# A down product with 20 products over four token tiles, three feature groups and two column halves, in a fused state-space and feed-forward kernel on one core

## The chip, the core and the metric

The kernel runs on one core of a Trainium2 chip. A core has five engines that each work through a list of instructions in order: TensorE (PE, matrix products; its weight loads are a row of their own, PEld), VectorE (DVE), ScalarE (ACT, functions from a table that has to be loaded), GpSimd (POOL) and SyncE (SP, which here only issues transfers). They wait for each other by semaphores. The metric is the device time of one execution in microseconds (us), less is better.

## What is computed

A chunked state-space recurrence (4 batches, 8 heads, 768 positions, head dimension 32, state 16) gives 3072 tokens of 256 values. These go through a feed-forward layer with 1536 hidden features, all in fp32:

```python
rms = np.sqrt(np.mean(x * x, axis=-1, keepdims=True) + 1e-06)
xn = x / rms * rms_g
g = xn @ w_gate                          # 256 x 1536
silu = g * (1.0 / (1.0 + np.exp(-g)))
val = xn @ w_val                         # 256 x 1536
return (silu * val @ w_out)              # 1536 x 256
```

The last product, hidden values by `w_out`, is called the down product here.

## The kernel before

Tokens are handled in six blocks of 512 (`TB`), hidden features in twelve tiles of 128. For each block there is a recurrence part (decays `L`, products `g`, states `S`, outputs `y`), a norm, the gate and value products, and the down product. The recurrence of block b + 1 runs between the products of block b.

**Block 0** starts while the weights are still arriving as words that have to be turned into numbers: fetch (transfer), pow (three functions on ACT, L182 to L185), man and wt (DVE), 20 pieces of each. It computes its first gates and values one feature tile after the other (L833, L843; silu_of L861 on ACT, hidden L866 on DVE) and its down product in the plain way, 12 steps `o.f` of four matmuls (`project`, L949).

**Gate and value products** of the other blocks, and of the second half of block 0, use a scheme with 7 products of 2x2 blocks (`product_gv`, L917): steps `P.k.j` (product k, pair j of feature tiles), `take` (copy out of PSUM by ACT, L923), `C` (sum by DVE, L929), `silu` (ACT, L938) and `hid` (product of gate and value by DVE, L942). The combined weights come from `combine_w` (step cw), the combined inputs from `combine_x` (step tx).

**The down product** of blocks 1 to 5 is the same kind of scheme for each of the six pairs j of feature tiles: 7 products `O.k.j`, each on two token tiles, so 84 matmuls of 128x128 by 128 a block (`product_o`, L1007). Steps s, s3, s2 and s4 form the sums of hidden values on DVE (`combine_h` L973, `difference_h` L977, `second_h` L980, `fourth_h` L983; 128x256 each), `two` the combined weights once. The products gather over j in four PSUM banks; `Otake` copies a bank on ACT (L1023) and `Oadd` adds on DVE into the output tile (L1034, and L1031 for the last block). The rows leave by halves or quarters of a block (`put_half`, `put_quarter`).

**The norm** of a block's tokens: sq (squares on ACT L748, added on POOL L751), ms (sum on PE, L783), rs (`norm_roots`: Ln and Exp on ACT, L792 and L793, and the store of the roots on SP), rb (four transfers that spread them, L801), xn (DVE, L810), tx (DVE), and then the next block's P.

**The order** is written by hand. A long string lists steps in the form block:kind.numbers, "/s" after a step names a PSUM slot, and the instructions of a step are issued where it stands; each engine takes its own in that order. The steps `table` and `exps` put a load of an ACT function table at a chosen place; where the next function is not in the loaded table, the compiler puts in a load by itself. PSUM is eight banks: three slots of two banks in block 0, of which slots 0 and 1 become the gate and val buffers (step `switch`), two banks for single uses, and slot 2 for y and g.

Of the kernel before, what the change touches and what calls it, by code (L numbers as in the profile page):

```python
# [20 lines left out]
def kernel(  # L21
# [796 lines left out]
    hs_ = {}  # L818

    def hidden_tile(blk, j):  # L820
        if (blk, j) not in hs_:
            hs_[blk, j] = ffn.tile([P, 2, 2, 256], FP32, tag="h", name="h", bufs=NF // 2)
        return hs_[blk, j]
# [23 lines left out]
    def of_block_0(f):  # L847
        return hidden_tile(0, f // 2)[:, f % 2].rearrange("p k m -> p (k m)")
# [28 lines left out]
    def combine_w(j):  # L877
        if j < NF // 4:
            s = raw.tile([P, 2, 4, P], FP32, tag="wr", name="sw", bufs=6)
        else:  # L880
            s = const.tile([P, 2, 4, P], FP32, name="sw%d" % j)
        Sw[j] = s
        f1, f2 = slice(2 * j * P, (2 * j + 1) * P), slice((2 * j + 1) * P, (2 * j + 2) * P)
        a11, a12, a21, a22 = wgv[:, :, 0, f1], wgv[:, :, 1, f1], wgv[:, :, 0, f2], wgv[:, :, 1, f2]
        for k, in0, in1, op in ((0, a21, a22, ALU.add), (1, s[:, :, 0], a11, ALU.subtract),
                                (2, a11, a21, ALU.subtract), (3, a12, s[:, :, 1], ALU.subtract)):
            nc.vector.tensor_tensor(out=s[:, :, k], in0=in0, in1=in1, op=op)
# [11 lines left out]
    def product_gv(blk, k, j):  # L899
# [10 lines left out]
        for w in range(2):  # L910
            if k in (1, 2):
                lhsT = wgv[:, w, k - 1, f1:f1 + P]
            elif k == 4:
                lhsT = wgv[:, w, 1, f2:f2 + P]
            else:
                lhsT = Sw[j][:, w, {5: 0, 6: 1, 7: 2, 3: 3}[k]]
            nc.tensor.matmul(out=dst[:, half[w]], lhsT=lhsT, rhs=rhs,  # L917
                             start=(k in (1, 2, 5) and w == 0), stop=True, skip_group_check=True)
# [21 lines left out]
    def hide_gv(blk, c, j):  # L940
        u, src = (us.pop(j), Xs[j]) if c == 21 else (cs[c, j][:, half[0]], cs.pop((c, j)))
        nc.vector.tensor_tensor(out=hidden_tile(blk, j)[:, c // 10 - 1, c % 10 - 1], in0=u,  # L942
# [5 lines left out]
    def project(blk, k, f, o, opens):  # L948
        nc.tensor.matmul(out=o, lhsT=hs_[blk, f // 2][:, f % 2, k // 2, (k % 2) * P:(k % 2 + 1) * P],  # L949
                         rhs=wo[:, f], start=opens, stop=(f == NF - 1), skip_group_check=True)  # L950

    Sh = {}

    two = {}

    def combine_wo(j0):
        js = slice(j0, j0 + 2)
        two[j0 // 2] = w = raw.tile([P, 4, 2, P], FP32, tag="wr", name="two", bufs=6)
        wop = wo.rearrange("p (j f) m -> p f j m", f=2)
        b11, b12, b21, b22 = [wop[:, f, js, m * P:(m + 1) * P] for f in range(2) for m in range(2)]  # L960
        for k, in0, in1 in ((0, b12, b11), (1, b22, w[:, 0]), (2, b22, b12),
                            (3, b21, w[:, 1])):
            nc.vector.tensor_tensor(out=w[:, k], in0=in0, in1=in1, op=ALU.subtract)

    def tiles_of_h(blk, j):
        h = hidden_tile(blk, j)
        return [h[:, f, :, a * P:(a + 1) * P] for a in range(2) for f in range(2)]


    def combine_h(blk, j):  # L970
        a11, a12, a21, a22 = tiles_of_h(blk, j)
        Sh[j] = s = ffn.tile([P, 2, P], FP32, tag="s", name="s", bufs=NF // 2)
        nc.vector.tensor_tensor(out=s, in0=a21, in1=a22, op=ALU.add)  # L973

    def difference_h(blk, j):
        a11, a12, a21, a22 = tiles_of_h(blk, j)
        nc.vector.tensor_tensor(out=a21, in0=a11, in1=a21, op=ALU.subtract)  # L977

    def second_h(blk, j):
        nc.vector.tensor_tensor(out=Sh[j], in0=Sh[j], in1=tiles_of_h(blk, j)[0], op=ALU.subtract)  # L980

    def fourth_h(blk, j):
        nc.vector.tensor_tensor(out=Sh[j], in0=tiles_of_h(blk, j)[1], in1=Sh[j], op=ALU.subtract)  # L983


    Os, ts, obs = {}, {}, {}

    def product_o(blk, k, j, ts=(0, 1)):
        bank_of = {1: "X", 6: "X", 7: "X", 2: 2, 4: 4, 5: 5, 3: 5}[k]

        apart = bank_of == 5 and blk == NBLK - 1
        if k in (1, 2, 4, 5) and j == 0:
            val = k in (2, 5)
            if apart:
                Os[5] = [bank("o", (P, P)) for t in ts]
            else:
                Os[bank_of] = later[val].tile([P, 512], FP32, tag="val" if val else "gate",
                                              name="o", bufs=2)
        o = Os[bank_of]
        a11, a12, a21, a22 = tiles_of_h(blk, j)  # L1000
        lhsT = {1: a11, 2: a12, 4: a22, 7: a21}[k] if k in (1, 2, 4, 7) else Sh[j]
        if k < 4:
            rhs = wo[:, 2 * j + (k > 1), (k // 3) * P:(k // 3 + 1) * P]
        else:
            rhs = two[j // 2][:, {4: 3, 5: 0, 6: 1, 7: 2}[k], j % 2]
        for t in ts:
            nc.tensor.matmul(out=o[t] if apart else o[:, t * P:(t + 1) * P], lhsT=lhsT[:, t],  # L1007
                             rhs=rhs, start=(k in (1, 2, 4, 5) and j == 0 and (apart or t == 0)),
                             stop=True, skip_group_check=True)

    def products_of_t(blk, k, t):
        for j in range(NF // 2):
            product_o(blk, k, j, (t,))

    def halves_of(o):
        return o[:, 0:2 * P].rearrange("p (t m) -> p t m", t=2)

    def taken_o(blk, k):
        if k == 1:
            ts[k] = nrm.tile([P, 2, P], FP32, tag="rest", name="v", bufs=1)  # L1020
        else:
            ts[k] = ffn.tile([P, 2, P], FP32, tag="v", name="v", bufs=2)
        nc.scalar.copy(out=ts[k], in_=halves_of(Os["X"]))  # L1023

    def total_o(blk, c, ts_=None):
        if blk not in obs:
            obs[blk] = ffn.tile([P, 2, 2, DM], FP32, tag="ob", name="ob", bufs=1)
        a, m, v, o = {11: (0, 0, 1, 2), 22: (1, 1, 7, 5), 21: (1, 0, 7, 4), 12: (0, 1, 6, 5)}[c]
        if isinstance(Os[o], list):
            for t in (0, 1) if ts_ is None else (ts_,):  # L1030
                nc.vector.tensor_tensor(out=obs[blk][:, t, a, m * P:(m + 1) * P], in0=ts[v][:, t],  # L1031
                                        in1=Os[o][t], op=ALU.add)
        else:
            nc.vector.tensor_tensor(out=obs[blk][:, :, a, m * P:(m + 1) * P], in0=ts[v],  # L1034
                                    in1=halves_of(Os[o]), op=ALU.add)

    def put_half(blk, a):
        dst = out[blk * TB:(blk + 1) * TB, :].rearrange("(t a p) m -> p t a m", t=2, a=2)
        nc.sync.dma_start(out=dst[:, :, a], in_=obs[blk][:, :, a])

    def put_quarter(blk, a, m, t=None):
        dst = out[blk * TB:(blk + 1) * TB, :].rearrange("(t a p) m -> p t a m", t=2, a=2)
        t, ms = slice(0, 2) if t is None else slice(t, t + 1), slice(m * P, (m + 1) * P)
        nc.sync.dma_start(out=dst[:, t, a, ms], in_=obs[blk][:, t, a, ms])

    def put(k):
        if k == 0:
            obs[0] = ffn.tile([P, NT, DM], FP32, tag="ob", name="ob", bufs=1)
        nc.scalar.copy(out=obs[0][:, k], in_=ps["o"][:, k % 2, k // 2])
        nc.sync.dma_start(out=out[k * P:(k + 1) * P, :], in_=obs[0][:, k])  # L1050
# [120 lines left out]
    def of_chunk(n, fn):  # L1171
# [4 lines left out]
        "s": combine_h, "s3": difference_h, "s2": second_h, "s4": fourth_h,  # L1176
        "O": product_o, "Otake": taken_o, "Oadd": total_o, "out": put_half,
        "Ot": products_of_t, "quarter": put_quarter,
        "cw": lambda blk, j: combine_w(j) if blk == 1 else None,
        "two": lambda blk, j: combine_wo(j) if blk == 1 else None,  # L1180
# [33 lines left out]
        0:sums.2 0:pow.6 0:fetch.8 0:wt.6 0:man.4 0:x.2 0:exp.3 0:early.1.0/1 0:rs.0 0:norm.0 0:xn.0  # L1214
        0:pow.4 0:wt.4 0:fetch.10 0:man.7 0:dT.3 0:turn.2 0:early.1.1 0:norm.1 0:rowout.0 0:exp.2
        1:table 0:man.9 0:silu.0 0:hid.0 0:gate.2/0 0:T.2 0:Tt.2.0 0:Tt.2.1 0:Td.2 0:pow.7
        0:fetch.14 0:wt.7 0:tx.0 0:gg.2/1 0:L1.2.2 0:L1.2.3 0:L.2.0 0:man.8 0:gate.3/2 0:pow.9
        0:fetch.11 0:silu.2 0:hid.2 0:pow.8 0:wt.9 0:wt.8 0:man.11 0:silu.3 0:hid.3 0:A.2 0:S.2
        0:x.3 0:pow.11 0:gate.4/1 0:silu.4 0:hid.4 0:cw.3 0:bc.3 0:scale.3 0:man.10 0:pow.12
        0:gate.5/0 0:silu.5 0:hid.5 0:pow.10 0:y.2/2 0:S.3 0:yt.2 0:sq.2 0:ydone.2 0:switch.1  # L1220
        0:P.2.3 0:switch.0 0:P.1.3 0:take.1.3 0:turn.3 0:T.3 0:Tt.3.0 0:Tt.3.1 0:wt.10 0:wt.11
        0:P.1.4 0:P.6.3 0:take.6.3 0:man.12 0:Td.3 0:man.13 0:pow.14 0:gg.3/2 0:L1.3.3 0:L.3.0
# [175 lines left out]
```

## Time and profile before

| | |
|---|---|
| median of 3 runs | 402.8 us (402.54 to 403.98) |
| the profiled execution | 404.32 us, its span 402.4 us |
| granted TensorE clock | 1.00 of full speed |
| PE from 81 to 385 us | 303.99 us busy of 304 |
| gate and value products L917 | 28% and 21% of the chain that ended last |
| down products L1007 | 24% of that chain |
| ACT table loads | 21 of 1.283 us each |

To read the profile: busy time of an engine is a sum over its instructions, and "x" is their number. The chain that ended last is followed back from the last instruction, at each step to what released it. A matmul in fp32 shows as two records. The duration of a matmul overlaps that of its neighbours, so what a further one costs is the time of a row of them divided by their number. PEclk is the clock that TensorE was granted. In a timeline, consecutive instructions of one line and form are put together: start, time, engine, line, operation, tiles, "x" how many, and in brackets the engine's idle time before it and what ended it.

### The profile page before, as it was taken

The numbers are of one execution on the slowest core, as the hardware profiler recorded it, in microseconds if no ns is written. First come the engines' busy times: TensorE is split into PE (matmuls) and PEld (weight loads), VectorE is DVE, ScalarE is ACT, GpSimd is POOL, SyncE is SP. The second block draws the span as 40 slices with busy tenths as digits, with TensorE's granted clock in tenths as the row PEclk, the third lists the DMA queues.
The fourth block names the chain that finished last, engine by engine and source line by source line (L and its number), as shares of the span: only waits on it lengthen the run. The fifth ranks groups of instructions, "written<-read, shape, count | busy, mean of one in ns | idle before, by whom it ended". The sixth has DMA issues, their size and how long they took to land.

```text
span 402.4 us, 9603 instructions
## 1 busy us (share of the span) xinstructions
PE 395.5 (98%) x3881; PEld 338.4 (84%) x3881; DVE 297.5 (74%) x686; ACT 228.2 (57%) x462; POOL 37.3 (9%) x57
## 2 busy tenths in 40 slices
PE   8989999999999999999999999999999999999997
PEld 5656467888888899888899988899988899988996
DVE  5899989999578897567689467886656667366871
ACT  2899788985675362743581663582645561345410
POOL 2210010001300022200103300021200010000000
PEclk9999999999999999999999999999999999999999
DMA  9897998219012216301223700202000001100001
GB/s 109 199 295 217 173 162 249 55 32 105 2 40 67 49 42 103 95 0 17 68 56 84 117 2 0 44 20 81 26 2 2 2 9 54 52 0 2 0 2 52
DMA packets 92596, 27.00 MB, mean 67 GB/s; under 512 B 77288, under 2 KB 86376, under 8 KB 92552
## 3 DMA queue, kind: packets, MB, share of 16 engines
q1 hardware_dynamic: 88392, 26.13, 29.2%
q10 hardware_dynamic: 4160, 0.26, 0.8%
q8 instruction: 30, 0.49, 0.5%
q14 instruction: 14, 0.11, 0.1%
HBM read 22.64 MB, written 3.74 MB: 66 GB/s over the span
## 4 chain that ended last, share of the span: by engine, by line
PE 93%; DVE 3%; ACT 3%; issue 1%; DVEq 0%
PE gate L917 28%; PE o L1007 24%; PE val L917 21%; PE o L949 5%; PE gate L833 4%; PE y L699 3%; PE g L562 1%; PE gate L843 1%; PE tp L505 1%; PE e L426 1%; PE y L627 1%; ACT L L455 0%; PE ms L783 0%; ACT e L183 0%; ACT e L185 0%
## 5 line engine op out<-in xcount | busy, mean ns | idle before, releaser
L929 DVE TENSOR_TENSOR c<-val,p 128x512 f32<-128x512 f32 x99 | 67.5, 688 | 33.5 <-PE val L917 29.3
L923 ACT COPY p<-gate 128x512 f32<-128x512 f32 x99 | 57.3, 581 | 52.5 <-PE gate L917 50.1
L917 PE MATMUL gate<-tx,sw 128*128 128x256 f32 x264 | 65.8, 381 | 0.0
L938 ACT ACTIVATE c<-c 128x256 f32<-128x256 f32 x99 | 39.4, 414 | 44.3 <-DVE c L929 44.2
L942 DVE TENSOR_TENSOR h<-c 128x256 f32<-128x256 f32 x99 | 41.0, 425 | 20.1 <-ACT c L938 20.1
L917 PEld LDWEIGHTS gate<-tx,sw 128*128 128x128 f32 x264 | 49.4, 190 | 7.2 <-issue 0.3
L917 PE MATMUL val<-xn,sw 128*128 128x256 f32 x132 | 33.5, 381 | 0.4 <-DVE c L929 0.4
L917 PE MATMUL val<-tx,sw 128*128 128x256 f32 x132 | 33.6, 382 | 0.1
L917 PE MATMUL val<-xn,wgv 128*128 128x256 f32 x132 | 33.7, 381 | 0.0
L917 PE MATMUL gate<-xn,wgv 128*128 128x256 f32 x132 | 33.3, 380 | 0.0
L917 PE MATMUL gate<-tx,wgv 128*128 128x256 f32 x132 | 32.9, 381 | 0.0
L475 POOL TENSOR_SCALAR_AFFINE_SELECT L<-L 64x512 f32<-64x512 f32 x32 | 23.7, 740 | 87.5 <-ACT L L473 77.9
L1007 PE MATMUL o<-wo,h 128*128 128x128 f32 x240 | 30.0, 276 | 0.0
L1007 PEld LDWEIGHTS o<-wo,h 128*128 128x128 f32 x240 | 28.5, 192 | 0.7 <-issue 0.2
L1007 PE MATMUL o<-two,h 128*128 128x128 f32 x240 | 28.9, 275 | 0.0
L1007 PE MATMUL o<-two,s 128*128 128x128 f32 x240 | 28.9, 275 | 0.0
L917 PEld LDWEIGHTS val<-xn,sw 128*128 128x128 f32 x132 | 24.8, 190 | 4.2 <-DVE c L929 0.8
L1007 PEld LDWEIGHTS o<-two,s 128*128 128x128 f32 x240 | 28.0, 192 | 0.4 <-issue 0.2
L917 PEld LDWEIGHTS val<-tx,sw 128*128 128x128 f32 x132 | 24.7, 190 | 4.0 <-DVE c L929 0.5
L1007 PEld LDWEIGHTS o<-two,h 128*128 128x128 f32 x240 | 27.8, 192 | 0.2 <-issue 0.2
L917 PEld LDWEIGHTS gate<-tx,wgv 128*128 128x128 f32 x132 | 24.8, 190 | 3.6 <-issue 0.4
L917 PEld LDWEIGHTS val<-xn,wgv 128*128 128x128 f32 x132 | 24.7, 190 | 3.5 <-issue 0.2
(192 smaller groups left out, 618.2 us busy)
## 6 DMA issues: line engine op xcount, KB each, us to landing
L<-rowd SPq DMA_DIRECT2D x32, 128.0 KB, 3.1
xr<-in_x_dram SPq DMA_DIRECT2D x24, 128.0 KB, 4.4
wr<-in_moe_w_out_dram SPq DMA_DIRECT2D x6, 512.0 KB, 5.9
wr<-in_moe_w_val_dram SPq DMA_DIRECT2D x5, 512.0 KB, 5.5
wr<-in_moe_w_gate_dram SPq DMA_DIRECT2D x5, 512.0 KB
out_dram<-ob SPq DMA_DIRECT2D x9, 256.0 KB, 2.2
br<-in_B_dram SPq DMA_DIRECT2D x22, 64.0 KB
cr<-in_C_dram SPq DMA_DIRECT2D x22, 64.0 KB, 2.4
```

The lines of the kernel that those rows point to most:

```text
L426: nc.tensor.matmul(out=e[:, i], lhsT=ident16, rhs=(whole16 if p < 2 else never16).unsqueeze(1).to_broadcast(m), start=True, stop=False, sk ...
L475: nc.gpsimd.affine_select(out=L[r], in_=L[r], pattern=[[0, NH], [1, HC]], compare_op=ALU.is_ge, fill=0.0, base=0, channel_multiplier=-1)
L505: nc.tensor.transpose(out=tp[:, k, i], in_=src[:, i].rearrange("p h n -> p (h n)"), identity=ident)
L699: nc.tensor.matmul(out=y[2 * k + u][rows, (2 * n + i) * HC:(2 * n + i + 1) * HC], start=(k, u, rows.start) not in opened, stop=True, skip_ ...
L833: nc.tensor.matmul(out=gv[:, k], lhsT=w[:, t, fs], rhs=xns[0][:, t], start=(t == 0), stop=(t == 1))
L917: nc.tensor.matmul(out=dst[:, half[w]], lhsT=lhsT, rhs=rhs, start=(k in (1, 2, 5) and w == 0), stop=True, skip_group_check=True)
L923: nc.scalar.copy(out=t, in_=Xs[j])
L929: nc.vector.tensor_tensor(out=t, in0=Zs[j], in1=a, op=ALU.add)
L938: nc.scalar.activation(out=u, in_=src[:, half[0]], func=AF.Silu)
L942: nc.vector.tensor_tensor(out=hidden_tile(blk, j)[:, c // 10 - 1, c % 10 - 1], in0=u, in1=src[:, half[1]], op=ALU.mult)
L949: nc.tensor.matmul(out=o, lhsT=hs_[blk, f // 2][:, f % 2, k // 2, (k % 2) * P:(k % 2 + 1) * P], rhs=wo[:, f], start=opens, stop=(f == NF - ...
L1007: nc.tensor.matmul(out=o[t] if apart else o[:, t * P:(t + 1) * P], lhsT=lhsT[:, t], rhs=rhs, start=(k in (1, 2, 4, 5) and j == 0 and (apar ...
```

## The change

The down product of blocks 1 to 5 is computed by another scheme. The 512 tokens are four tiles (rows 1 to 4), the twelve feature tiles are four instances of three groups, and the 256 columns are two halves. 20 products of combined factors, each summed over the four instances, replace the 24 of the plain way: 20 x 4 = 80 matmuls of 128x128 by 128 a block. All hidden values lie in one tile `hid` of `const`. `O.k.h` issues two of a product's four instances.

```diff
+    hid = const.tile([P, NF, 2, 256], FP32, name="hid")
...
-        for k, in0, in1, op in ((0, a21, a22, ALU.add), (1, s[:, :, 0], a11, ALU.subtract),
...
+        for o, in0, in1, op in ((s[:, 0], a21, a22, ALU.add), (s[:, 1], s[:, 0], a11, ALU.subtract),
+                                (a21, a11, a21, ALU.subtract), (s[:, 2], a12, s[:, 1], ALU.subtract)):
...
+    KG, NG3 = 3, NF // 3
...
+    COMBOS = [("2", "b12", "b11"), ("8", "b21", "b31"), ("13", "b22", "b21"),
...
+    SUMS = [("2", "a41", "a11"), ("1", "a12", "+a13"), ("a12", "a12", "a22"),
...
+    def sum_h(blk, n, engine=nc.vector):
+        o, in0, in1 = SUMS[n]
+        engine.tensor_tensor(out=hidden_or_sum(o), in0=hidden_or_sum(in0),
...
+    PLACES = {2: (0, 0), 15: (0, 1), 0: (0, 2), 4: (0, 3), 6: (1, 0), 16: (1, 1), 8: (1, 2),
+              13: (1, 3), 11: (2, 0), 12: (2, 1)}
+    SECOND = {3: 2, 7: 6, 17: 15, 19: 16, 9: 0, 18: 4, 5: 8, 1: 11, 10: 12, 14: 13}
...
+    def product_o(blk, k, h):
+        b, place = PLACES[SECOND.get(k, k)]
+        if (blk, b) not in Os:
+            Os[blk, b] = later[b > 0].tile([P, 512], FP32, tag="val" if b else "gate",
+                                           name="o", bufs=2)
+        u, v = FACTORS[k]
+        for g in (2 * h, 2 * h + 1):
...
+            nc.tensor.matmul(out=Os[blk, b][:, place * P:(place + 1) * P],
+                             lhsT=hidden_or_sum(u)[:, g], rhs=rhs,
+                             start=(blk, b) not in opened, stop=True, skip_group_check=True)
...
+    TOTALS = [(2, "c-41"), (6, "c+32"), (15, "c+22"), (16, "c+31"), (3, "c-11"), (17, "c+12"),
...
+        if first:
+            if what[0] == "+":
+                nc.scalar.copy(out=o, in_=src)
+            else:
+                nc.scalar.activation(out=o, in_=src, func=AF.Copy, scale=-1.0)
+        else:
+            nc.vector.tensor_tensor(out=o, in0=o, in1=src,
+                                    op=ALU.add if what[0] == "+" else ALU.subtract)
+
+    def put_tile(blk, i, m=None):
...
+        "u": sum_h, "up": lambda blk, n: sum_h(blk, n, nc.gpsimd), "O": product_o, "w": total_o, "put": put_tile,
...
+        "two": lambda blk, n: combine_wo(n),
+        "twop": lambda blk, n: combine_wo(n, nc.gpsimd),
```

In words: the 16 sums of hidden values of a block are 128x512 each and partly replace hidden values in place; a step `u` makes one on DVE, `up` on POOL. The twelve combined weights are made once (`two` on DVE, `twop` on POOL) and lie in five different places, one of them the fourth slice of the gate weights' tiles, which `combine_w` frees by writing one of its sums over a part of `wgv`. Products gather in places of 128 columns in three PSUM banks. Ten products open a place and the ten in `SECOND` add onto one of them, after the first one has been read. 26 output terms `w.n` read the places: 8 copy on ACT (those with a "c", as many as there are parts of the output), 18 add or subtract on DVE. Each of the four token tiles leaves by its own transfer (`put`).

The string of steps is new from the 150th step on. In block 0 this is where it starts:

```diff
-        0:sums.2 0:pow.6 0:fetch.8 0:wt.6 0:man.4 0:x.2 0:exp.3 0:early.1.0/1 0:rs.0 0:norm.0 0:xn.0
-        0:pow.4 0:wt.4 0:fetch.10 0:man.7 0:dT.3 0:turn.2 0:early.1.1 0:norm.1 0:rowout.0 0:exp.2
-        1:table 0:man.9 0:silu.0 0:hid.0 0:gate.2/0 0:T.2 0:Tt.2.0 0:Tt.2.1 0:Td.2 0:pow.7
+        0:sums.2 0:pow.6 0:fetch.8 0:wt.6 0:man.4 0:x.2 0:pow.4 0:man.9 0:wt.4 0:rowout.0 0:rs.0
+        0:norm.0 0:exp.3 0:pow.9 0:early.1.0/1 0:tok 0:exp.2 1:exps 0:fetch.10 0:early.1.1 0:xn.0
+        0:silu.0 0:wt.9 0:tx.0 0:turn.2 1:dT.1 0:T.2 0:Tt.2.1 0:gate.2/0 0:Tt.2.0 0:Td.2 0:tokout
```

Block 0's last down steps `o.f` now stand among the products of block 1. A part of block 2's down stage in the new string:

```
2:up.3 2:u.1 2:up.4 2:silu.22.5 2:rs 3:turn.0 2:C.12.5 2:hid.22.5 2:O.15.0 2:O.15.1 2:w.0 2:w.2
2:P.3.4 2:hid.12.2 2:up.2 2:C.12.4 2:O.3.0 2:O.3.1 2:silu.12.5 3:bc.1 3:dT.0 2:hid.12.5 2:u.5
```

## The prediction

> **What bounds the kernel now.** I read the page's busy shares first, then the chain, then a table by stretch, then what stands around the few places where TensorE (PE) waits.
>
> ```profile
> PE 395.5 (98%) x3881; PEld 338.4 (84%) x3881; DVE 297.5 (74%) x686; ACT 228.2 (57%) x462; POOL 37.3 (9%) x57
> PEclk9999999999999999999999999999999999999999
> PE 93%; DVE 3%; ACT 3%; issue 1%; DVEq 0%
> L1007 PE MATMUL o<-wo,h 128*128 128x128 f32 x240 | 30.0, 276 | 0.0
> ```
>
> PE is busy for 98% of the span at the full granted clock, and 93% of the chain that ends last is PE's. So PE's work is the time, as long as the others keep up. Do they, everywhere? The table by stretch (us, then PE, weight load, VectorE (DVE), ScalarE (ACT), GpSimd (POOL) busy, clock, DMA share, GB/s):
>
> ```profile
> 31.00:57.50 26.50, 25.70 (x292) 14.87 (x291) 25.85 (x58) 23.38 (x41) 0.00 (x0) 1.00 0.86 166
> 57.50:81.00 23.50, 22.99 (x278) 18.51 (x277) 21.96 (x53) 20.19 (x42) 1.95 (x2) 1.00 0.56 165
> 81.00:139.70 58.70, 58.70 (x453) 51.16 (x452) 47.58 (x105) 37.69 (x74) 5.65 (x8) 1.00 0.28 47
> ```
>
> From 31 to 81 us DVE and ACT are nearly as full as PE (25.85 and 23.38 of 26.5 us): a microsecond added there to either can reach PE. From 81 to 395 us PE shows no idle time, and the others have slack (DVE 47.58 of 58.7). So the change is judged in two regions: block 0, and the stages at the ends of blocks 1 to 5.
>
> **What goes.** The mean of a down matmul's record in the page (276 ns) overlaps its neighbours. The pitch is what counts, and the chain's longest piece gives it:
>
> ```profile
> 152.62 8.04 PE o L1007 x72
> ```
>
> 8.04 / 72 = 0.1117 us a record. A block's down product had 6 pairs x 7 products x 2 token tiles = 84 matmuls of 128x128x128, and now has 20 products x 4 instances = 80. An fp32 matmul shows as two records: 840 become 800 over five blocks. PE's other instructions are the same in number (2171 to 2151 in all). **40 x 0.1117 = -4.47 us**, if nothing opens a gap. That is all that there is to gain.
>
> **DVE, ACT and POOL in a down stage.** Before, DVE did 24 sums of 128x256 a block (51.2 us over five blocks) and the output sums (8.2 us): 11.9 us a block. After, DVE has 47 of the 80 sums of 128x512. Their pitch is 0.60 us, from other 128x512 sums: 5.7 us a block. Of 26 output terms, 18 stay on DVE, 16 at 0.286 (L1031) and two wide at 0.42: 5.4. Together 11.1, so DVE is no fuller. POOL gets 33 sums; its 128x512 addition took 1.268 us in the middle (0.735 to 1.449): +42 us over five blocks, on an engine that was 9% busy. ACT gets 40 copies of 128x128 at 0.263 (L518) and loses 15 of 128x256 at 0.371: +4.9 us. The compiled programs also differ in ACT's table loads: 21 become 37. A load is 1.283 us: 16 x 1.283 = +20.5 us, on an engine that was idle for 43% of the span. What these cost is decided by where they stand.
>
> **Block 0, from the 150th step on.** ACT was here:
>
> ```profile
> 34.00 1.00 ACT L455 ACTIVATE L<-e 128x1024 f32<-128x1024 f32 x1
> 35.02 1.28 ACT L1196 ACT_TABLE_LOAD   x1
> 36.31 0.63 ACT L861 ACTIVATE u<-u 128x512 f32<-128x512 f32 x1
> 36.85 0.35 ACT L516 COPY T<-tp 128x256 f32<-128x256 f32 x1
> 37.10 0.84 ACT L1115 ACTIVATE T<-tp,tmask 128x256 f32<-128x256 f32 x2
> ```
>
> The copies of T end at 37.9 us. I walked the new list with the old durations. From 29.44 (behind pow.6): pow.4 2.18, rs.0 1.26, exp.3 1.02, pow.9 2.18, exp.2 1.02, two loads 2.57 (the step that computes exponentials to fetch their table now stands where it is already there), silu.0 0.54, T and Tt 0.99: 41.3 us, +3.4. Behind T stand Td.2 on DVE, then PE's state products. The old order used the same time for the weights of later gates, so part comes back. The same walk further on: silu.4 behind pow.11 ends at 55.4, so P.2.3 starts at about 56.1 (before 54.4); take.1.3 behind a load, pow.12 and yt.2 ends at 60.55, and P.6.3 waits for it (60.6 against 58.6); P.1.5, ms.1 and P.7.5 lose 1.0 to 1.3 each behind wt.14, sq.3 and the loads of rs.1, partly the same loss again. There are 8 loads up to there, where there were 4. By the walk, block 0's last gate product ends at 89.8. The old list reached the same work at 93.15 - 6.9 (four o.f products that now stand later) + 0.44 (a turn) = 86.7. **Term: +3.1 us.** Bounds: 0, if PE finds other work (it lost only 0.80 us at 56.4 and 0.44 at 65.9 there before), and 8 x 1.283 = 10.3, if every load up to there cost its length; four more loads than before, 5.1, is the nearer upper end. I take the walk.
>
> At this place a page bears on the sum. The Trainium skill, "ScalarE: Activation LUTs", section "What ACT_TABLE_LOAD costs", puts a drain of about 1380 ns beside the 1283 ns of the load, some 2.66 us a switch. The rows above show the 1.283 and no drain: the load starts at 35.02, the next function at 36.31. By the page block 0's four additional loads would cost 4 x 1.38 = 5.5 us more, an estimate; by the trace nothing, and the sum goes by the trace.
>
> **Ends of blocks 1 to 5.** The first output term of a place is now a copy on ACT, and the second product of that place waits for it, since it adds onto the same PSUM. Queued before these copies on ACT is rs (ln 0.37, exp 0.31), with a table load before each: 3.25 us. Walked: in block 2 the copies w.0 and w.2 come 0.85 late for O.3; in block 3 w.1 and w.3, behind a redundant load and rs, 0.8 late for O.8; in block 4 O.8 0.4; block 1 nothing; block 5 0.35 (its last sums alternate POOL, DVE, POOL, and O.10 waits for the last). **Term: +2.4 us.** Bounds: 0, for before such pairs of loads stood in the stages too (204.64 and 206.66, 265.86 and 267.54) while PE was busy for all of 203 to 226 and 262 to 288; and two loads in each of five stages, 10 x 1.283 = 12.8. PE queues in order, so behind a waiting O stands everything. I take the walk, near the low end, because most products do not wait for a copy.
>
> The transfers count for little: the roots' store and four loads keep their place behind rs (5.3 us from rs to xn), the output goes as four 128 KB stores a block instead of halves, and the last store follows the last DVE sum either way:
>
> ```profile
> 399.47 0.29 DVE L1031 TENSOR_TENSOR ob<-v,o 128x128 f32<-128x128 f32 x1 [1.05 <-PE o L1007]
> ```
>
> From there to the end of the span (402.4) is 2.6 us, and that stays. The hidden values now lie in one tile for all blocks, and a block's first hid waits for the last O product before it, O.10. In the new lists six to eight P products stand on PE between O.10 and the product that this hid multiplies, so the wait is over when it comes up: 0, and no row gives it another end.
>
> **Sum.** -4.47 + 3.1 + 2.4 = **+1.0 us**. The profiled execution took 404.32 (span 402.4 and 1.9 around it), 1.5 over the median of the runs, 402.8. Laid on the median: **403.8 us**. A measurement of this kernel can tell about 0.5% (2.0 us) from no change, so that is no change: 400.8 to 404.8. The forecast's own range, with the walks off by 2.5 either way, is 401.3 to 406.3.
>
> **Rivals.**
>
> *Faster: the loads are hidden.* Between 81 and 385 us 18 loads cost PE nothing (303.99 us busy of 304). If PE's queue has enough ready products in front of each wait, only some 0.5 us is left of the 5.5: 402.8 - 4.5 + 0.5 = 398.8. For it speaks the slack of ACT (21 of 58.7 us); against it the tight stretch 31 to 81 us.
>
> *Slower: POOL and DVE hold each other up.* One place of the old trace shows it, the all-engine timeline at 144.6 us:
>
> ```profile
> 144.63 1.83 DVE L973 TENSOR_TENSOR s<-h 128x256 f32<-128x256 f32 x2
> 144.72 1.45 POOL L751 TENSOR_TENSOR sq<-sq 128x512 f32<-128x512 f32 x1 [34.29 <-issue]
> ```
>
> and the times of that line, least, middle and most:
>
> ```profile
> L973 DVE TENSOR_TENSOR s<-h x30: 414/420/1495, 126.7 to 385.2; 128x256 f32<-128x256 f32 x30
> ```
>
> One DVE sum took 1495 instead of 420 ns beside POOL's: +1.07 us. That agrees with the Trainium skill, "SBUF — State Buffer", section "🔬 SBUF: two separate sides", by which DVE with two SBUF inputs and GpSimd take one shared port in turn, each for a whole instruction. After the change a down stage has some 6.6 POOL sums. If each stops a DVE sum, DVE gets 6.6 x 1.07 = 7 us more in a stage of 80 x 2 x 0.1117 = 17.9 us, where it has 11.1 of sums, and the hid products of the last pairs besides (some 4 us): 22 us, 4 over the stage. It decides from the point where DVE's and POOL's work in a stage, one behind the other, passes PE's. Most sums are made ahead of need, so I count about 1 us lost a stage, 5 in all: 403.8 + 5 = 408.8. For it speak 33 POOL sums in the chain of sums; against it that sums from PSUM beside POOL kept their time (1.28 for two at 199.28, POOL running from 199.75).
>
> *It does not do what it says.* PE's count falls by exactly the 20 matmuls, so this is out.
>
> **Chances.** Forecast 0.45 (of it 0.32 within 0.5%, 0.12 above, 0.01 below); loads hidden, 0.33, faster; POOL against DVE, 0.17, slower; the page's drain, 403.8 + 5.5 = 409.3, 0.05, slower. Faster 0.34, same 0.32, slower 0.34. The range leaves out a tenth on each side: 398.3 (all of the 4.5 kept) to 409.
>
> **What would show it.** The records of the down product fall to 800 at the same 0.11 us. Walks right: PE idle of 2 to 4 us between 31 and 90 us, put down to ACT's T, take or silu copies, and idle PE of up to 0.9 us ahead of O.3 or O.8 released by ACT. Faster rival: PE busy 391 and the span 398. POOL rival: sums of hidden values at 1.3 us or more beside POOL's, and PE waiting for DVE in the down stages. I am wrong if PE is idle over 6 us, or waits for transfers.

## The result and the profile after

The changed kernel took 407.93 us in the median of 6 runs (406.81 to 408.38), the kernel before 403.0 beside it: 1.0116 of the time before, 95% interval 1.0097 to 1.0135. That is 4.9 us slower. The forecast was 403.8, taken as no change, with 401.3 to 406.3 for its own walks and an outer range up to 409.0. The two profiled executions lie 3.9 us apart (spans 402.4 and 406.3).

The page of the changed kernel:

```profile
PE 393.9 (97%) x3841; PEld 333.3 (82%) x3841; DVE 305.7 (75%) x681; ACT 249.6 (61%) x503; POOL 88.0 (22%) x93
PE 73%; ACT 17%; DVE 7%; issue 2%; DVEq 0%; ACTq 0%
```

PE's records fall by 40, as counted, and its busy time by 1.6 us. But its idle time (span less busy) grows from 6.9 to 12.4 us: 5.5 - 1.6 = 3.9. The second line points at ACT: its share of the chain that ended last went from 3% to 17%, though ACT is busy for only 61% of the span. The table by stretch of the changed kernel (us, then PE, weight load, DVE, ACT, POOL busy, clock, DMA share, GB/s):

```profile
31.00:95.00 64.00, 58.86 (x614) 41.80 (x613) 57.63 (x129) 60.54 (x105) 1.94 (x2) 1.00 0.76 162
...
140.00:395.00 255.00, 253.92 (x2540) 228.13 (x2534) 179.27 (x387) 134.69 (x298) 61.99 (x53) 1.00 0.15 34
```

The same stretches in the kernel before:

```profile
31.00:95.00 64.00, 62.70 (x635) 45.71 (x634) 60.90 (x138) 55.63 (x101) 1.95 (x2) 1.00 0.65 141
...
140.00:395.00 255.00, 254.99 (x2523) 231.45 (x2522) 174.76 (x389) 124.50 (x264) 23.27 (x28) 1.00 0.16 35
```

In 31 to 95 us PE lost 62.70 - 58.86 = 3.84 us of work, while ACT became fuller (55.63 to 60.54) and DVE emptier. From 140 to 395 us it lost 1.07. PE's waits in the changed kernel name the releasers (us in total, times, longest):

```profile
PE gate L912 <- ACT p L918: 1.5, 2, 0.9
PE g L562 <- DVE hid L849: 1.1, 1, 1.1
...
PE gate L912 <- DVE hid L937: 1.1, 1, 1.1
PE o L1033 <- ACT ob L1060: 1.0, 3, 0.4
...
PE tp L505 <- ACT yt L767: 0.8, 1, 0.8
PE o L1033 <- DVE ob L1064: 0.4, 1, 0.4
```

All but one stand where the walk of the prediction put them: the state products g (42.85 us), P.6.3 behind take.1.3 (60.71), P.1.5 behind hid.21.3 (72.07), the turn behind yt.3 (76.54; the walk named ms.1, a few steps on), P.7.5 behind take.6.5 (82.61), and O.3 or O.8 behind the copies of blocks 2 to 4 (210.8, 280.3, 338.0). The exception is the last line: in block 5 it is O.1 that waits, for an output sum on DVE (w.18, 399.4), where the walk had named O.10.

How ACT came late is read off its timeline ahead of T:

```profile
36.83 1.28 ACT L1222 ACT_TABLE_LOAD   x1
38.12 1.28 ACT L856 ACT_TABLE_LOAD   x1
39.42 0.63 ACT L856 ACTIVATE u<-u 128x512 f32<-128x512 f32 x1
39.95 0.36 ACT L516 COPY T<-tp 128x256 f32<-128x256 f32 x1
40.20 0.84 ACT L1141 ACTIVATE T<-tp,tmask 128x256 f32<-128x256 f32 x2
```

The first of the two loads brings a table that is there already. T ends at 41.0 (forecast 41.3, before 37.9). The products g are put down to hid.0 on DVE, but DVE had itself waited for ACT's T, and hid.0 stood behind that (42.02 to 42.70 us):

```profile
41.08 0.42 DVE L536 TENSOR_TENSOR T<-tp,dT 128x256 f32<-128x256 f32 x1 [1.09 <-ACT T L1141]
```

And in block 2, ahead of the first two output copies (L1062, L1060):

```profile
207.12 1.28 ACT L792 ACT_TABLE_LOAD   x1
208.41 0.37 ACT L792 ACTIVATE r<-ms,eps 128x128 f32<-128x128 f32 x1
208.80 1.28 ACT L793 ACT_TABLE_LOAD   x1
210.09 0.31 ACT L793 ACTIVATE r<-r 128x128 f32<-128x128 f32 x1
210.31 0.26 ACT L1062 ACTIVATE ob<-o 128x128 f32<-128x128 f32 x1
210.47 0.26 ACT L1060 COPY ob<-o 128x128 f32<-128x128 f32 x1
```

Ln and Exp each fetch a table of their own, and O.3 waits for the copies that stand behind them.

### The profile page after: what moved, and what is told of

Read it like the earlier page. It is cut to its first block, busy times and chain, and to the rows that moved or that the text cites. A ratio compares the mean times of both kernels' runs of the same rounds, so it can differ in the third digit from the quotient of the medians.

```text
span 406.3 us, 9652 instructions
## 1 busy us (share of the span) xinstructions
PE 393.9 (97%) x3841; PEld 333.3 (82%) x3841; DVE 305.7 (75%) x681; ACT 249.6 (61%) x503; POOL 88.0 (22%) x93
## 4 chain that ended last, share of the span: by engine, by line
PE 73%; ACT 17%; DVE 7%; issue 2%; DVEq 0%; ACTq 0%
PE gate L912 24%; PE o L1033 21%; PE val L912 17%; PE gate L828 3%; PE y L699 2%; ACT e L183 1%; ACT e L182 1%; ACT e L185 1%; DVE c L924 1%; PE g L562 1%; DVE hid L937 1%; ACT p L918 1%; ACT c L933 1%; ACT L792 1%; ACT L933 1%
## 5 line engine op out<-in xcount | busy, mean ns | idle before, releaser
L912 PE MATMUL gate<-tx,wgv 128*128 128x256 f32 x264 | 66.2, 382 | 1.1 <-ACT p L918 0.9
L937 DVE TENSOR_TENSOR hid<-c 128x256 f32<-128x256 f32 x99 | 45.4, 475 | 16.4 <-ACT c L933 16.3
L912 PEld LDWEIGHTS gate<-tx,wgv 128*128 128x128 f32 x264 | 48.9, 190 | 9.2 <-ACT p L918 2.5
L1064 DVE TENSOR_TENSOR ob<-ob,o 128x128 f32<-128x128 f32 (+1 forms) x90 | 24.0, 298 | 19.4 <-PE o L1033 15.9
L1033 PE MATMUL o<-two,hid 128*128 128x128 f32 x280 | 36.9, 277 | 0.0
L1033 PEld LDWEIGHTS o<-two,hid 128*128 128x128 f32 x280 | 34.4, 192 | 1.4 <-DVE hid L937 0.7
L1007 POOL TENSOR_TENSOR s<-hid 128x512 f32<-128x512 f32 x10 | 13.2, 1323 | 98.9 <-DVE hid L937 94.6
L912 PE MATMUL gate<-tx,sw 128*128 128x256 f32 x132 | 33.1, 382 | 0.6 <-ACT p L918 0.6
L912 PEld LDWEIGHTS gate<-xn,wgv 128*128 128x128 f32 x132 | 24.4, 190 | 5.2 <-ACT p L918 1.2
L912 PEld LDWEIGHTS gate<-tx,sw 128*128 128x128 f32 x132 | 24.4, 190 | 4.8 <-ACT p L918 1.4
```

The lines of the kernel that those rows point to most:

```text
L912: nc.tensor.matmul(out=dst[:, half[w]], lhsT=lhsT, rhs=rhs, start=(k in (1, 2, 5) and w == 0), stop=True, skip_group_check=True)
L937: nc.vector.tensor_tensor(out=hid[:, 2 * j + c // 10 - 1, c % 10 - 1], in0=u, in1=src[:, half[1]], op=ALU.mult)
L1007: engine.tensor_tensor(out=hidden_or_sum(o), in0=hidden_or_sum(in0), in1=hidden_or_sum(in1), op=ALU.add if in1[0] == "+" else ALU.subtract)
L1033: nc.tensor.matmul(out=Os[blk, b][:, place * P:(place + 1) * P], lhsT=hidden_or_sum(u)[:, g], rhs=rhs, start=(blk, b) not in opened, stop= ...
L1064: nc.vector.tensor_tensor(out=o, in0=o, in1=src, op=ALU.add if what[0] == "+" else ALU.subtract)
```

## The experiments

**Theory A**: the new order makes ACT late, in block 0 and ahead of the output copies. **Rival B**: POOL's sums stop DVE's in the down stages. **Rival C**: the loads are covered and the order of the other steps costs. PE's busy time from 31 to 95 us serves as the gauge of block 0: 62.70 before, 58.86 in the changed kernel. What a gap costs is counted from the start of one matmul to the start of the next, beyond their pitch; this is 0.16 to 0.2 us more than the idle time that the profile shows (the 1.08 us at 72.07 cost 1.28). So counted, PE's gaps from 31 to 95 us add up to 6.3 us, before to 2.0.

**1. The old order of block 0, the new down product.** The changed kernel with the old string up to the first sum of hidden values, then all steps of the new string that are not done yet:

```diff
-0:sums.2 0:pow.6 0:fetch.8 0:wt.6 0:man.4 0:x.2 0:pow.4 0:man.9 0:wt.4 0:rowout.0 0:rs.0
+0:sums.2 0:pow.6 0:fetch.8 0:wt.6 0:man.4 0:x.2 0:exp.3 0:early.1.0/1 0:rs.0 0:norm.0 0:xn.0
...
```

> The new down product, but block 0 and the first half of block 1's gate and value products in the old order (up to the first sum of block 1); from there the new order. Theory A (the time is lost where ACT comes late: 6.3 us of PE gaps between 31 and 95 us, 2.0 in the old kernel; the down stages lose 3.5): about 4.3 less than the changed kernel's 407.9, so 403.6, and PE's gaps between 31 and 95 us come back to about 2 us. Rival B (POOL's and DVE's sums hold each other up in the down stages): no change, 407 to 408, since all 33 POOL sums stay.

Measured: 416.37, ratio 1.0335 (1.0312 to 1.0359). The gauge says 62.70, so block 0 loses nothing in its old order; but the seam between the two strings lost more than that: PE waits 3.6 us at 131 and 7.3 us at 140 us. The first wait stands behind DVE, which had waited 4.19 us for a transfer of decays (rowd). Ahead of the second, ACT loads four tables in 6.7 us (at 132.37, 134.09, 136.03 and 137.76), because silu and decay exponentials take turns there, and the copy that PE waits for comes behind them. As a time the run decides nothing; it left a finding on the clock, below.

**2. The new order of block 0, the old down product.** The kernel before with the new string up to its first O, then the rest of the old one:

```diff
-0:sums.2 0:pow.6 0:fetch.8 0:wt.6 0:man.4 0:x.2 0:exp.3 0:early.1.0/1 0:rs.0 0:norm.0 0:xn.0
+0:sums.2 0:pow.6 0:fetch.8 0:wt.6 0:man.4 0:x.2 0:pow.4 0:man.9 0:wt.4 0:rowout.0 0:rs.0
...
```

> The other half alone: the old down product with its 84 matmuls a block, behind block 0 in the new order. Theory A: 403.0 + 4.3 = 407.3, with the same gaps of PE between 31 and 95 us as the changed kernel. Rival B: 403, as there are no POOL sums.

Measured: 410.53, ratio 1.0186 (1.0164 to 1.0209). The gauge says 58.69, with gaps at the same places to within 0.3 us of time. So block 0's loss belongs to its order and not to the product. Not all of the 7.9 us is block 0's: at the seam there is a gap of 1.61 us (145.9 us), and the rest was not taken apart.

**3. The wasted table loads taken out, the order kept.**

```diff
-0:norm.0 0:exp.3 0:pow.9 0:early.1.0/1 0:tok 0:exp.2 1:exps 0:fetch.10
+0:norm.0 0:exp.3 0:pow.9 0:early.1.0/1 0:tok 0:exp.2 0:fetch.10
...
-2:silu.22.5 2:rs
+2:silu.22.5 2:exps 2:rs
```

> The changed kernel with the same order, but each exps step moved to just ahead of rs (one load there instead of two) and the table steps taken out, all of which stood where their table was loaded already or is loaded anyway: 20 table loads instead of 37. Theory A, in its form that the loads are what makes ACT late: the gaps of block 0 shrink from 6.3 to 1 to 2 us, and the waits for ACT's copies in blocks 2 to 4 (1.9 us) go: 401.5 to 403.5. Rival C (the loads are hidden, the order of the steps itself is what costs): 407 to 408. Rival B: 407 to 408.

Measured: **401.28**, ratio 0.996 (0.9944 to 0.9976) to the kernel before. 6.65 us came back from 17 loads (6.3 by the two ratios), and the kernel is now slightly faster than the one before. Of the 4.47 us that the count promised it keeps some 1.4; its trace shows the early gate of block 0 waiting 1.28 us for ACT's exp.3 (33.21 us) and O.1 in the last block still waiting for w.18. ACT's share of the chain that ended last is 3% again. The page's first line, the stretch, and ACT ahead of block 2's copies:

```profile
PE 390.8 (98%) x3841; PEld 331.7 (83%) x3841; DVE 306.7 (77%) x681; ACT 228.1 (57%) x486; POOL 89.0 (22%) x93
```

```profile
31.00:95.00 64.00, 62.13 (x632) 45.26 (x631) 61.64 (x138) 56.21 (x106) 1.46 (x2) 1.00 0.79 165
```

```profile
201.16 1.28 ACT L1222 ACT_TABLE_LOAD   x1
202.45 0.37 ACT L792 ACTIVATE r<-ms,eps 128x128 f32<-128x128 f32 x1
202.85 0.31 ACT L793 ACTIVATE r<-r 128x128 f32<-128x128 f32 x1
203.66 0.28 ACT L1062 ACTIVATE ob<-o 128x128 f32<-128x128 f32 x1 [0.50 <-PE o L1033]
```

ACT's busy time falls by 21.5 us (17 x 1.283 = 21.8), the gauge is back at 62.13, and the copy now waits 0.50 us for PE instead of O.3 for the copy. As causes of the 4.9 us, rivals B and C fall with this run: the same sums on POOL, the same order of the steps that compute.

**4. POOL's sums on DVE.**

```diff
-        "u": sum_h, "up": lambda blk, n: sum_h(blk, n, nc.gpsimd),
+        "u": sum_h, "up": lambda blk, n: sum_h(blk, n),
...
-        "twop": lambda blk, n: combine_wo(n, nc.gpsimd),
+        "twop": lambda blk, n: combine_wo(n),
```

> The changed kernel with the 33 hidden sums and 3 weight sums of POOL on DVE instead, at the same places. Theory A: DVE gets 6.6 x 0.6 = 4 us more a stage and is no longer stopped by POOL: within 1 us of 407.9 if the stage has room, up to 3 us more if not. Rival B: 1 us a stage comes back, 402.9.

Measured: 424.55, ratio 1.0527 (1.0497 to 1.0558), 16.6 us slower than the changed kernel. Its waits show whom POOL had relieved:

```profile
PE o L1033 <- DVE s L1007: 7.0, 7, 2.1
PE o L1033 <- DVE hid L1007: 3.1, 3, 1.5
```

B has the wrong sign, and theory A's bound (up to 3 us more) was too small by far. Each O waits for a sum that waits for others; that DVE has less room in that chain than its busy time over a whole stage says (76% of the span) is the likely reading, and no further run tested it.

**5. The first try with the seam put earlier**, at the first product of block 1: the old string up to the step 0:ex.11 just ahead of it.

```diff
-0:sums.2 0:pow.6 0:fetch.8 0:wt.6 0:man.4 0:x.2 0:pow.4 0:man.9 0:wt.4 0:rowout.0 0:rs.0
+0:sums.2 0:pow.6 0:fetch.8 0:wt.6 0:man.4 0:x.2 0:exp.3 0:early.1.0/1 0:rs.0 0:norm.0 0:xn.0
...
```

> As the first try with the old order of block 0, but the seam is put earlier, at the first product of block 1, where the two orders have done nearly the same work. Theory A (ACT comes late in block 0's new order): PE's gaps between 31 and 95 us are the old kernel's 2 us instead of 6.3, the stages keep theirs: 403.6, up to 1 more from the seam. Rival (block 0's order costs nothing, the stages do): 407 to 408.

Measured: 410.82, ratio 1.019 (1.0165 to 1.0215). Again the gauge says 62.70, and the seam loses: PE is busy for 40.25 of the 45 us from 95 to 140. The two strings could not be joined without a loss at either place, so as a time this run decides nothing either; runs 6 and 7 part the change in another way.

**6. and 7. The wasted loads out of block 0 alone, and out of the later blocks alone.** Run 6 takes out the four steps of this kind in block 0 and puts one ahead of rs.1; run 7 does it for the other steps:

```diff
-0:ms.1 0:rs.1
+0:ms.1 1:exps 0:rs.1
...
-2:silu.22.5 2:rs
+2:silu.22.5 2:exps 2:rs
```

> The changed kernel with the wasted table loads taken out in block 0 alone (5 loads fewer, 32). Theory A with loads as the cause: the gaps of block 0 fall from 6.3 to some 1.8 us, as they did when all wasted loads went: 407.9 - 4.4 = 403.5. If the gain of that run came from the stages: 406 to 408.

> The other part alone: exps just ahead of rs in blocks 1 to 4, no other exps or table step there (25 loads), block 0 as it is. The waits of O.3 and O.8 for ACT's copies in blocks 2 to 4 (1.9 us with the restarts) go: 407.9 - 2.2 = 405.7, so that both parts add up to the 6.6 us measured together. If the parts overlap or the waits pass on to DVE: 407.

Measured: 404.05, ratio 1.002 (1.0001 to 1.0039), and 406.23, ratio 1.0072 (1.0053 to 1.0092). That is 3.9 and 1.7 us less than the changed kernel. The gauge says 62.26 and 58.47, so each edit acts where it was made. Together they give 5.6 of the 6.65 that both gave in one kernel; run 10 shows a wait that may hold part of the rest.

**8. The kernel before without its wasted loads.** Its table steps go, and each exps stands ahead of rs:

```diff
-1:table 0:man.9 0:silu.0
+0:man.9 0:silu.0
...
-3:ms 3:rs
+3:ms 3:exps 3:rs
```

> The kernel before, with its own wasted loads taken out in the same way (16 loads instead of 21). Theory A: its loads were covered (PE busy for 303.99 of 304 us from 81 us on, gaps of 2 us between 31 and 81 us that end on ACT's squares and DVE's sums): 402 to 403. Rival: every wasted load costs its 1.28 us in either kernel: 5 x 1.28 = 6.4 less, 396.

Measured: 403.44, ratio 1.0009 (0.9996 to 1.0021). No change, and PE's busy times in the two stretches (62.70 and 254.99) are the same to the last digit: in the old order the same kind of load stands where ACT has time. On ACT each load takes its 1.283 us; what it costs the kernel is decided by its place.

**9. Two waits that run 3 had left.** On top of run 3:

```diff
-0:x.2 0:pow.4 0:man.9 0:wt.4 0:rowout.0 0:rs.0 0:norm.0 0:exp.3 0:pow.9 0:early.1.0/1
+0:x.2 0:exp.3 0:early.1.0/1 0:rs.0 0:norm.0 0:xn.0 0:pow.4 0:man.9 0:wt.4 0:rowout.0 0:pow.9
...
-5:w.7 5:u.12 5:O.12.0
+5:w.7 5:w.18 5:u.12 5:O.12.0
```

> The changed kernel without the wasted loads, with two steps more: exp.3 with its early gate, and rs.0 with the norm and xn, stand ahead of pow.4 again as in the old order (ACT's exp.3 was 1.3 us late for the early gate there), and the last block's w.18 stands ahead of O.12 (O.1 waited 0.54 us for it). Theory A: 401.3 - 1.2 to 1.8 = 399.5 to 400.1, faster than both kernels. If the early gate only waits elsewhere afterwards: 400.8 to 401.3.

Measured: 401.38, ratio 0.9973 (0.9958 to 0.9989): as run 3, so a miss. The wait for exp.3 is gone and others stand in its place, 0.38 us at 36.14 and this one:

```profile
41.28 0.48 PE L562 MATMUL g<-T 32*64 32x128 f32 x16 [1.05 <-DVE hid L849]
```

The early gate started sooner, but the state products still wait for hid.0 behind T, whose place on ACT had not moved. The gauge fell from 62.13 to 61.66.

**10. One load alone taken out**, the one at 36.83 us.

```diff
-0:exp.2 1:exps 0:fetch.10
+0:exp.2 0:fetch.10
```

> The changed kernel with one table load taken out, the redundant one ahead of block 0's first silu (at 36.83 us); its five neighbours stay. Theory A says that the losses along block 0 add up: the 1.18 us gap ahead of the state products at 42.85 goes and nothing later takes it back: 406.7. If the later waits (60.7, 72.1, 76.5, 82.6 us) absorb it, since ACT is then behind for its own reasons: 407.5 to 408.

Measured: 407.37, ratio 1.0112 (1.0088 to 1.0135); this lies between the two expectations, and against the changed kernel's interval it can't be told from no change. In its trace the gap at 42.85 is gone and every later gap up to the 280th microsecond stands some 1.2 us earlier, so the later waits did not absorb the gain. Some 0.3 us of it stood there ahead of the removed load already (at 38.1 us), since this execution had begun faster (see the last section); for the same reason the early gate waits 1.35 us in it, and the gauge, 58.59, shows no gain. Then, in this execution, a new gap of 1.43 us takes it back:

```profile
284.25 1.41 DVE L810 SCALAR_TENSOR_TENSOR xn<-yt,gcol,sq 128x512 f32<-128x512 f32 x2 [2.36 <-DMA sq<-roots]
285.05 1.13 PE L912 MATMUL gate<-xn,wgv 128*128 128x256 f32 x4 [1.27 <-DVE xn L810]
```

Block 4's first products wait for xn, and xn for the spread roots: the last of their four transfers landed 3.6 us after its issue. Run 6's trace has the same gap (1.16 us at 281.7; 3.3 us to landing). In the changed kernel's own trace the transfer took 1.9 us, DVE waited 0.67 us there, and PE none.

**11. Four redundant loads put into block 0 of the kernel before.**

```diff
+1:exps 1:table 0:man.9 0:silu.0
...
+2:table 0:take.1.3
...
+2:table 0:yt.3
...
+2:table 0:take.6.5
```

> The kernel before, with four redundant table loads put into its block 0 on ACT: ahead of the silu before T, ahead of take.1.3, ahead of yt.3 and ahead of take.6.5 (25 loads instead of 21). Theory A (block 0 has no room on ACT, so a load there reaches PE): 4 x 1.28 = 5.1 us less the idle time that ACT has between them (0.5 to 0.8 us at a time): 2.5 to 4.5 more, 405.3 to 407.3. Rival (the loads are covered, as in the later blocks): under 0.6 more, 403.3.

Measured: 405.31, ratio 1.0064 (1.0045 to 1.0082), 2.7 us more, at the low end of theory A. The new waits are those behind two of the four:

```profile
PE tp L505 <- ACT yt L767: 1.1, 1, 1.1
PE gate L917 <- ACT p L923: 0.8, 1, 0.8
```

The gauge falls to 60.79. This is the mechanism in the other kernel, by an edit that changes nothing else; behind the loads ahead of T and of take.6.5 PE shows no wait.

## Why the prediction was right, and where its sizes were off

The time lies in the outer range, near its slow end, and the mechanism is that of the forecast's walks: ACT's loads, put where PE has no work ready. The size is not. The forecast said no change, and 407.9 lies outside the 401.3 to 406.3 that it gave its own walks; the range holds it because it was drawn for the rivals too. The time alone spoke for the POOL rival (408.8) rather than for the forecast (403.8), and only the runs tell them apart. Its own sign of being wrong, PE idle over 6 us, can't be decided as it stands: PE was idle for 6.9 us before already, and for 5.5 more after. By the forecast's steps:

**What goes, 4.47 us.** The pitch is the same (a long row of the new products from the chain):

```profile
213.26 8.93 PE o L1033 x80
```

8.93 / 80 = 0.1116. But the times from each down product's record to PE's next start, block 0's included, add up to 115.2 us before and 114.0 after: 1.2 less, so 3.3 were given back.

**Block 0, forecast +3.1.** Measured: +4.3 (6.3 us of gaps where there were 2.0; 3.8 by the gauge). Removing five loads there gave 3.9 back. The places were right: T ended 0.3 us from the forecast (whose listed terms add up to 41.2, not 41.3), P.6.3 started at 60.71 where 60.6 was forecast, P.1.5 and P.7.5 lost 1.28 and 1.08 where 1.0 to 1.3 was. The walk then counted these as partly the same loss again; the trace shows that they add up.

**Ends of blocks, forecast +2.4.** Measured: +3.4. That is the 3.3 above, less 0.6 for the wait for xn at 94 us, which belongs to block 0, plus 0.2 and 0.5 for breaks ahead of an O at 207.1 and 210.8 us, which that sum leaves out. The loads were 1.7 of it (run 7). The waits were smaller than forecast in blocks 2 and 3 (0.49 and 0.46 instead of 0.85 and 0.8) and larger in block 4 (0.57 instead of 0.4); in the last block 0.54 instead of 0.35, at another step than the one walked. What the walk left out are short breaks: at 20 places in the down products, before at 8, PE's next start comes 0.2 us after the last instead of 0.11, without a wait that the profile shows (at a change to another kind of matmul, and between some O products): 1.2 us. With these terms the sum is -4.5 + 4.3 + 3.4 = 3.2 of the 3.9 between the traces; what is left are smaller gaps, one of 0.3 us at 136.3 among them.

**DVE, forecast no fuller.** Measured: 297.5 to 305.7 us busy. Beside POOL's sums, DVE's hid products (L937) and hidden sums (L1007) took 9.2 us more in all than at their middle times; in run 4, with no hidden sums on POOL, 2.5.

**The median.** The forecast laid the sum on the median of the runs; the traces differ by 3.9, the medians by 4.9. The traces offer a reason, and no run tested it: PE's first ten microseconds come in two forms (last section), and both profiled executions had the longer one. With the shorter one the old order is 1.5 us ahead by the turn at 57 us (run 8's trace, 55.75 instead of 57.23), while the new order meets ACT's exp.3 at the early gate and keeps some 0.5 (33.21 in run 3, 33.31 in run 10, 33.80 in the changed kernel). Which form the executions without a trace had is not on record. Also, xn's wait for the roots shows in some traces only.

**The rivals.** "Loads are hidden" was wrong for the new order and right for the loads that the old one has (run 8). The forecast's argument against it, the tight stretch from 31 to 81 us, was what decided. POOL against DVE happens: here two hid products took 2.30 us instead of 0.76 beside POOL's sums, which follow each other from 208.18 to 212.78 us.

```profile
208.18 1.78 POOL L1007 TENSOR_TENSOR hid<-hid 128x512 f32<-128x512 f32 x1 [3.19 <-DVE hid L937]
...
209.34 2.30 DVE L937 TENSOR_TENSOR hid<-c 128x256 f32<-128x256 f32 x2
```

It agrees with the rule that the prediction named from the Trainium skill, "SBUF — State Buffer", section "🔬 SBUF: two separate sides". But PE's waits in the down stages are for ACT's copies and DVE's output sums, and POOL's share of the sums saves more than it costs (run 4).

The drain that the Trainium skill, "ScalarE: Activation LUTs", section "What ACT_TABLE_LOAD costs", puts beside a load is not to be seen: the loads at 36.83 and 38.12 follow each other in 1.29 us, and the silu starts 1.30 after the second. Its section "Table sets" says that ln and exp share one set, so that one load serves both; the trace agrees only where that set was asked for ahead of rs (run 3: one load at 201.16), while the changed kernel loaded twice (207.12 and 208.80).

## What to carry to other kernels

A count of fewer matmuls is worth its pitch only if every wait that the new order brings is walked, above all on an engine that looks half idle: ACT was busy for 61% of the span and PE still waited for it. Look at function table loads by their place: the same 1.28 us was free in one place (five loads, run 8) and cost 0.8 us a load in another (five loads, run 6), and a preload that stood right ahead of its user became waste when the steps around it were moved. When an order has been laid out anew, check first which of its loads bring what is already there.

## What the runs showed of the hardware

**A long wait costs more than its length.** In the first experiment PE waited 3.6 us until 131.14 and 7.3 us until 140.21. Behind the first of these waits its granted clock was halved, and it stayed so until 145 us:

```profile
131.00:140.20 9.20, 1.78 (x52) 1.38 (x52) 7.88 (x12) 8.37 (x11) 6.04 (x7) 0.52 0.14 36
140.20:145.20 5.00, 4.99 (x12) 4.01 (x13) 2.52 (x5) 2.14 (x4) 1.25 (x2) 0.52 0.00 0
145.20:156.00 10.80, 10.80 (x301) 9.43 (x300) 8.79 (x20) 4.21 (x11) 3.04 (x2) 1.00 0.17 28
```

The twelve records of the second stretch came at 0.43 us each instead of 0.216, 2.5 us more. The length of a wait alone does not tell: in run 4 the clock fell behind a wait of 1.85 us (292.90; 0.57 from 293 to 297 us), while it stayed at 1.00 behind 2.05 us in the same trace (359.20) and behind 2.12 us in run 5 (112.58). In the traces of the two kernels, with waits of up to 1.1 us, it stayed at 1.00 throughout.

**PE's first ten microseconds come in two forms,** whatever the kernel. In the traces of the two kernels each pair of matmuls d_ps (L379, at 7.09 and 7.73 us) took 0.85 us, in run 8's 0.49, with a clock of 1.00 in the rows of both. The first turn (L511) started at 10.57 us before and at 8.56 in run 8. Runs 2, 4, 6 and 7 have the longer form, runs 1, 3, 5 and 8 to 11 the shorter. So two traces are compared with care: 2 us of difference can stand there before anything that was changed begins.
